# Routing of four batches in fuller loop steps, and a rule on when an expert slot may begin: top-k attention followed by a mixture of experts on one core

## The chip, the cores and the metric

One core of a Trainium2 chip runs one program. The metric is the device time of one execution in microseconds, as the median of several runs. The engines are named as the profile names them: PE (TensorE, matmuls; PEld its weight loads), DVE (VectorE), ACT (ScalarE), POOL (GpSimd), SP (SyncE, which here issues DMAs; SPq is its queue).

## The reference

Attention over 8 batches, 8 heads, 576 rows and 64 columns keeps the 32 highest scores of each row. Its output, as 4608 rows of 512, goes through a router and then, each row through one of 8 experts:

```python
scores = scale * np.matmul(q, k.transpose(0, 1, 3, 2))
kth = np.partition(scores, -top_k, axis=-1)[..., -top_k:-top_k + 1]
mask = scores >= kth
scores = np.where(mask, scores, -1000000000.0)
...
logits = x @ w_gate + modality_bias[modality_id]
e_idx = np.argmax(logits, axis=1)
...
    h = np.maximum(x[mask] @ w1[e], 0.0)
    out[mask] = gate_w[mask, None] * (h @ w2[e])
```

## The kernel before, in words

**The main loop.** The scores are cut into 288 tiles of 128 x 576 (a pair of heads has 9, a batch 36). A main loop of 310 steps, numbered i, is software-pipelined over the tiles. In step i PE makes the scores of tile i+2 (L396), ACT copies them to SBUF as Ssb (L404), DVE takes the eight largest of each of seven parts of tile i (MAX8, L411), merges those of tile i-1 (L420 to L424), and searches tile i-5 once more (`find`, L453) in the product y that POOL made of scores and signs (L449). From a count of signs and three small steps (L460 to L462) the 32nd value follows, and DVE's L473 (`keep`) makes the masked, unnormalised row P of tile i-7. Behind each L473 stands a gate on POOL (L477): a copy of one element of P, so that POOL starts the next y only when that L473 is over. PE transposes P (L488), ACT copies it (L496), and PE multiplies with V (L516).

**Routing.** When a batch's 36 tiles are done, its logits are made on PE and summed on DVE (L582 to L590). Then `route` (L592) gives a list of small steps: softmax and arg max on DVE (L627 to L635), ranks within the expert by a few small matmuls (L607 to L611), two products on POOL (L640, L641), the gate weight and the row's place in a sorted list on DVE (L642 to L646), then bookkeeping. POOL divides each row block by its softmax sum in halves (L556, 80 in all) and scatters each of the batch's five blocks of rows to the list xs in DRAM by an indirect DMA (L620, `SEND` below). `count_up` (L649) adds the batch's counts, `done` says that the batch is counted (`seen`).

The loop takes these steps from a queue `side`, at most `SN` = 4 to a loop step, and puts them behind that step's DVE work, each between two other instructions where there are any. A `PAUSE` in the queue ends the loop step's share, so that what follows stands in the next loop step. For the first `EB` batches the count comes before the scatters, which wait in `sendq` and leave one to a loop step; for the others the scatters come first and the count last. The two kinds also place logits and row blocks at different loop steps of the 36 (`RLF`, `RLM`, `RL` and `RXF`, `RXM`, `RX`, L1241).

**Expert slots.** A slot is 256 rows of one expert: rows xg are loaded from xs (L732), transposed (L791), multiplied with w1 (L803) and w2 (L815) and scattered to the output (L830, an indirect DMA on POOL). Which expert comes next is decided on the chip by some ten small DVE steps (L703 to L723). Where slots pause for want of counted rows, `more_moe` (L877) begins anew when a batch has been counted: it puts those picks, the w1 loads (L751), the xg load, three or two `PAUSE`s and the token step (L743 on DVE, or L740 on POOL) into a queue `rush`, of which at most `RN` = 6 go into a loop step. A slot's PE work (36 pieces) is dealt out over the loop steps by a budget in `spare_pe`: each step adds `STEP` = 3.3 and takes off what attention costs. Until the first slot begins, `keep_warm` (L928) gives PE dummy matmuls (L931). Slots that are not done in the loop follow behind it, in `slot` (L1005), with matmuls of another form.

SP issues its DMAs in the program's order: loads of k, q and v, the copies of ks and qs for the next pair of heads (L316, L318), weights and xg.

Of the kernel before, what the change touches and what calls it, by code (L numbers as in the profile page):

```python
# [26 lines left out]
SN = 4  # L27
# [23 lines left out]
PB = 6  # L51
COST = {"trans": 0.5, "qk": 0.5, "mix": 1.12, "rest": 0.22, "t": 0.11, "prep": 0.43, "logits": 1.2, "xrow": 0.54, "av": 0.42, "av8": 0.17}
RN = 6
QO = 0
EB = 3
RLF = (0, 1)
RXF = (3, 4, 5, 6, 7)
RLM = (3, 4)
# [12 lines left out]
def kernel(  # L71
# [14 lines left out]
    B, H, S, D = q.shape  # L86
# [4 lines left out]
    NT = NPAIR * 9  # L91
# [23 lines left out]
    PAUSE = lambda: None  # L115
# [284 lines left out]
    def sevac(i, parts=False):  # L400
        T[i]["S"] = sb = wk.tile([128, S], FT, name="Ssb", bufs=LR + 1 + QL - QO)
        sv = sb.rearrange("p (a b) -> p a b", a=2)
# [190 lines left out]
    def route(lg, bias, oh, x5b, early=False):  # L593

        t5 = lambda nm: const.tile([128, 5], FT, name=nm)
        t40 = lambda nm: const.tile([128, 5, E], FT, name=nm)
        bc = lambda t: t[:, :, None].to_broadcast([128, 5, E])
        be = lambda t: t[:, None, :].to_broadcast([128, 5, E])
        l2, z, key, ez, pr, pb = t40("r_l2"), t40("r_z"), t40("r_key"), t40("r_ez"), t40("r_pr"), t40("r_pb")
        mx, km, sm, ps5 = t5("r_mx"), t5("r_km"), t5("r_sm"), t5("r_ps5")  # L600
        dest = const.tile([128, 5], I32, name="dest")
        st = {}

        def ranks():
            ps = psX.tile([128, 6, E], FT, name="X")
            st["ps"] = const.tile([128, 6, E], FT, name="r_rk")
            PE.matmul(ps[:, 0:5, :], tri, oh, start=True, stop=False, skip_group_check=True)  # L607
            for c in range(1, 5):
                PE.matmul(ps[:, c:5, :], onesb, oh[:, 0:5 - c, :], start=False, stop=False, skip_group_check=True)
            for c in range(5):  # L610
                PE.matmul(ps[:, 5, :], onesb, oh[:, c, :], start=(c == 0), stop=(c == 4), skip_group_check=True)  # L611
            A.activation(st["ps"], ps, AF.Copy)

        def total():
            assert not behind
            V.tensor_reduce(ps5, pr, axis=AX.X, op=OP.add)

        def send(c):
            n_ = 128 if c < 4 else 64
            apart(G.indirect_dma_start(  # L620
                out=xs[:ZROW, :], out_offset=bass.IndirectOffsetOnAxis(ap=dest[:n_, c:c + 1], axis=0),
                in_=x5b[:n_, c, :], in_offset=None), scat, reads)
            if not early:
                fresh.append(scat[-1])

        return [
            lambda: V.tensor_tensor(l2, lg, bias, op=OP.add),  # L627
            lambda: V.tensor_reduce(mx, l2, axis=AX.X, op=OP.max),
            lambda: V.tensor_tensor(z, l2, bc(mx), op=OP.subtract),
            *[PAUSE] * EZP,  # L630
            lambda: A.activation(ez, z, AF.Exp),
            lambda: V.scalar_tensor_tensor(key, z, 0.0, be(rev), op0=OP.is_equal, op1=OP.mult),
            lambda: V.tensor_reduce(km, key, axis=AX.X, op=OP.max),
            lambda: V.tensor_tensor(oh[:, 0:4, :], key[:, 0:4, :], bc(km)[:, 0:4, :], op=OP.is_equal),
            lambda: V.tensor_tensor(oh[:64, 4, :], key[:64, 4, :], km[:64, 4:5].to_broadcast([64, E]),  # L635
                                    op=OP.is_equal),
            *[PAUSE] * RKP,
            ranks,
            PAUSE,
            lambda: on_pool(lambda: G.tensor_tensor(pb, st["ps"][:, 0:5, :], be(base), op=OP.add)),  # L640
            lambda: on_pool(lambda: G.tensor_tensor(pr, pb, oh, op=OP.mult)),  # L641
            lambda: V.tensor_reduce(sm, ez, axis=AX.X, op=OP.add),  # L642
            lambda: V.tensor_scalar(sm, sm, EPS, None, op0=OP.add),
            lambda: V.reciprocal(x5b[:, :, GW], sm),
            total,
            lambda: V.tensor_scalar(dest, ps5, float(ZROW), None, op0=OP.add),  # L646
            lambda: G.tensor_scalar(x5b[:, :, TOK], tokb, 1.0, 1.0, op0=OP.mult, op1=OP.mult),
            lambda: G.tensor_scalar(tokb, tokb, float(S), 1.0, op0=OP.add, op1=OP.mult),
        ], [lambda c=c: send(c) for c in range(5)], lambda: V.tensor_tensor(base, base, st["ps"][:, 5, :], op=OP.add)  # L649
# [208 lines left out]
    rush = deque()  # L858
    moe = deque()
    puts = deque()  # L860
    xev = deque()
    seen = [0]
    nslot = [0]
# [10 lines left out]
    plan = {"ready": -1, "go": False}  # L874
    quiet = set()

    def more_moe():  # L877

        n = nslot[0]
        b = seen[0] // S  # L880
        full = 2 * b
        fits = lambda x: x >= PB
        if plan["ready"] == n:
            if moe or not plan["go"]:
                return
            chores()
            nslot[0] += 1
            nxt = full >= n + 2
            moe.extend(expert(n, True, nxt, fits(n + 1), True))
            if nxt:  # L890
                plan.update(ready=n + 1, go=True)
        elif full >= n + 1:
            now = SL[n - 1] if moe else {"xt": True, "used": [4, 4]}
            if not now["xt"]:
                return
            plan.update(ready=n, go=False)
            pick, rows, done, tok = sched(n, fits(n))
            free = []

            def begin():  # L900
                free.extend(now["used"])
                now["nxt"] = True

            def take(x, g):
                return lambda: (load_w1, load_w2)[x](n, g) if g < free[x] else None
            l1 = [lambda: [take(0, g)() for g in range(4)]]
            l2 = [take(1, g) for g in range(4)]
            go = [lambda: plan.update(go=True)]
            lead = l1 + [WAIT] + rows if sendq else rows + l1
            rush.extend(pick + [begin] + lead + done + [PAUSE] * (3 if b < 2 else 2) + tok + go)  # L910
            quiet.update(l2)
            side.extend([f for x in l2 for f in (x, PAUSE)])
# [152 lines left out]
    for i in range(LAST):  # L1065
# [13 lines left out]
        if ok(i + QL):  # L1079
            cost += COST["mix" if (i + QL) % 9 == 8 else "qk"]  # L1080
        if QO == 0:
            scores()
# [12 lines left out]
        while nxt:  # L1095
            nxt.popleft()()
        if ok(i + QL) and QO == 0:
            sevac(i + QL)
# [20 lines left out]
        if 0 <= b1 < B:  # L1119
            if r == 0:  # L1120
                chore.extend(recip(b1, den[b1 % 2]))
            rl, rx = (RLF, RXF) if b1 in (0, B - 1) else (RLM, RXM) if b1 < EB else (RL, RX)
            if r == rl[0]:
                rows_of[b1] = logits(b1, xTs(b1))
                cost += COST["logits"]
            if r == rl[1]:
                logit_rows(b1, rows_of[b1], lgb[b1 % 2], later if 0 < b1 < EB else late)
                cost += COST["xrow"]
# [4 lines left out]
            def done(n=b1 + 1):  # L1133
                seen[0] = n * S
                fresh.clear()
            if r == rl[1] + (3 if 0 < b1 < EB else 2):
                steps, sends, count_up = route(lgb[b1 % 2], bias_all[:, b1], ohb[b1 % 2], x5, b1 < EB)
                side.extend(steps)
                if b1 < EB:
                    side.extend([count_up, done, lambda x=sends, n=5 * b1: sendq.extend((c, f, n + c) for c, f in enumerate(x))])  # L1140
            if b1 >= EB and r == max(rl[1], rx[4]) + 3:
                side.extend([f for x in sends for f in (x, PAUSE)] + [count_up, done])
# [7 lines left out]
        spare_pe = min(spare_pe + (STEP if i < NT + TL + END[0] else END[1]) - cost, CAP)  # L1150
        while seen[0] and spare_pe > 0:
            if i < NT + ME:
                more_moe()
            if not moe:
                break
            c, f, new = moe[0]
            if new and after:
                break
            moe.popleft()
            f()  # L1160
            spare_pe -= c
        if QO == 1:
            scores()
# [13 lines left out]
        for x, f in enumerate(lo):  # L1177
            b_.insert(LOP[x] if x < len(LOP) else len(b_), f)
        small_ = []
        for x in range(RN if rush else 0):  # L1180
            if rush and rush[0] is WAIT and sendq:
                break
            f = rush.popleft() if rush else PAUSE
            if f is PAUSE:
                break
            small_.append(f)
        if not small_:
            while bulk and not PJ[1] < j <= PJ[2]:
                chore.append(bulk.popleft())
            while chore:  # L1190
                small_.append(chore.popleft())
        for x in range(SN - len(small_)):
            if side and side[0] in quiet and PJ[1] < j <= PJ[2]:
                break
            f = side.popleft() if side and not rush else PAUSE
            if f is PAUSE:
                break
            small_.append(f)
# [208 lines left out]
```

## Time and profile before

| | |
|---|---|
| median of 3 runs | 1256.58 us (1254.93 to 1257.7) |
| the profiled execution | 1256.33 us |
| its span, first to last instruction | 1254.5 us |
| mean granted PE clock | 0.983 |
| busy, of the span | PE 1182.1 us (94%), DVE 1156.4 (92%), ACT 1018.0 (81%), POOL 687.8 (55%) |

A row of instructions in order of time has: start us, duration us, engine, line, operation, output<-inputs, shapes, count, and in brackets the engine's idle time before it and what ended it. A row that sums a line's instructions has their durations in ns as least/median/most and the first and last start in us. Busy time is not the same as time that counts: an engine that isn't waited for costs nothing, and an instruction that is held up by another engine's access shows as a long duration, not as idle time.

### The profile page before, as it was taken

What the parts mean: (1) busy time and instruction counts of PE and PEld (TensorE: products, weight loads), DVE (VectorE), ACT (ScalarE), POOL (GpSimd) and SP (SyncE); (2) the same over time, 40 slices, a digit from 0 to 9 for tenths busy, and PEclk for the clock granted to TensorE, in tenths of its full rate; (3) what the DMA queues carried; (4) which work ended last, traced back from release to release, by engine and by line L of the source; (5) the groups of instructions that cost most, each with busy time, mean ns of one, the idle gap of its engine ahead of it and who ended that gap; (6) DMA issues with size and microseconds to landing.
All of it is one profiled execution on the core that took longest, in us unless ns stands there. A gap on an engine that the chain in (4) does not pass through costs nothing. (4 is left out here: it accounts for less than half of the span.)

```text
span 1254.5 us, 29230 instructions
## 1 busy us (share of the span) xinstructions
PE 1182.1 (94%) x8141; PEld 929.6 (74%) x8141; DVE 1156.4 (92%) x5827; ACT 1018.0 (81%) x2042; POOL 687.8 (55%) x1342
## 2 busy tenths in 40 slices
PE   7888888899999999999999999999999999899995
PEld 6666676776868677786867777787868766799894
DVE  5999999999999999999999999999999995866764
ACT  4899988889989998988988988898889885555553
POOL 3555558456765576656865676556766772511110
PEclk8899998999999999999999999999999999999998
DMA  6665334775477557565476466666586423777563
GB/s 132 161 177 124 87 87 130 189 195 156 92 204 211 135 151 198 164 170 137 128 219 175 121 186 192 183 158 165 135 240 162 125 93 101 232 242 269 196 217 124
DMA packets 210133, 205.80 MB, mean 164 GB/s; under 512 B 106365, under 2 KB 155517, under 8 KB 209952
## 3 DMA queue, kind: packets, MB, share of 16 engines
q1 hardware_dynamic: 202384, 183.61, 54.1%
q0 software_dynamic: 6208, 19.54, 4.4%
q8 instruction: 70, 1.15, 0.4%
q14 instruction: 111, 0.91, 0.2%
q10 hardware_dynamic: 1360, 0.59, 0.2%
HBM read 123.35 MB, written 24.23 MB: 118 GB/s over the span
## 5 line engine op out<-in xcount | busy, mean ns | idle before, releaser
L411 DVE MAX8 cand<-Ssb 128x8 f32<-128x82 f32 (+1 forms) x2016 | 430.8, 231 | 8.9 <-ACT Ssb L404 8.9
L449 POOL TENSOR_TENSOR y<-Ssb,K 128x576 f32<-128x576 f32 x288 | 366.8, 1274 | 4.7 <-ACT K L443 4.1
L396 PE MATMUL S<-ks,qs 128*128 128x288 f32 x1016 | 232.9, 352 | 34.4 <-ACT Ssb L404 25.0
L404 ACT ACTIVATE Ssb<-S 128x576 f32<-128x576 f32 (+1 forms) x289 | 189.2, 655 | 72.0 <-PE S L396 53.0
L443 ACT ACTIVATE K<-Ssb,n 128x576 bf16<-128x576 f32 x288 | 227.8, 791 | 13.0 <-POOL y L449 12.5
L396 PEld LDWEIGHTS S<-ks,qs 128*128 128x128 f32 x1016 | 158.1, 193 | 91.9 <-issue 39.7
L467 ACT ACTIVATE ex<-Ssb,sm 128x576 f32<-128x576 f32 x288 | 226.1, 785 | 0.0
L453 DVE MAX8 mg<-y 128x8 f32<-128x576 f32 x288 | 214.6, 745 | 2.1 <-POOL y L449 2.1
L473 DVE SCALAR_TENSOR_TENSOR P<-Ssb,kth,ex 128x576 f32<-128x576 f32 x256 | 213.7, 835 | 0.6 <-PE T L488 0.3
L496 ACT ACTIVATE PT<-T 128x640 f32<-128x640 f32 (+1 forms) x288 | 191.5, 665 | 8.1 <-PE T L488 8.1
L803 PE MATMUL E<-xgT,w1b 128*128 128x256 f32 x768 | 188.3, 387 | 4.6 <-ACT xgT L784 2.4
L815 PE MATMUL E<-w2b,hT 128*128 128x512 f32 x384 | 182.7, 600 | 0.7 <-ACT hT L807 0.3
L488 PE MATMUL T<-idf,P 128*128 128x128 f32 x1152 | 170.1, 275 | 0.0
L803 PEld LDWEIGHTS E<-xgT,w1b 128*128 128x128 f32 x768 | 139.3, 191 | 31.1 <-ACT xgT L784 3.9
L477 POOL TENSOR_SCALAR spare<-P 1x1 f32<-1x1 f32 x256 | 47.8, 187 | 207.9 <-DVE mg L422 191.1
L516 PE MATMUL X<-PT,vm 128*64 128x256 f32 (+1 forms) x1536 | 147.8, 335 | 3.5 <-ACT st L279 2.5
L488 PEld LDWEIGHTS T<-idf,P 128*128 128x128 f32 x1152 | 136.5, 141 | 3.5 <-issue 1.3
L436 POOL TENSOR_SCALAR n<-mg 128x1 f32<-128x1 f32 x288 | 65.9, 229 | 109.1 <-DVE mg L424 100.8
L516 PEld LDWEIGHTS X<-PT,vm 128*64 128x64 f32 x1536 | 85.8, 137 | 50.4 <-issue 16.6
L815 PEld LDWEIGHTS E<-w2b,hT 128*128 128x128 f32 x384 | 66.5, 190 | 54.2 <-issue 50.5
L556 POOL TENSOR_TENSOR x<-x,rd 128x256 f32<-128x256 f32 (+1 forms) x80 | 53.8, 678 | 27.8 <-ACT x L560 27.8
L443 ACT ACTIVATION_READ_ACCUMULATOR K<-Ssb,n 128x1 f32 x288 | 61.5, 213 | 0.0
(208 smaller groups left out, 2248.7 us busy)
## 6 DMA issues: line engine op xcount, KB each, us to landing
w1b<-in_moe_w_dram SPq DMA_DIRECT2D x80, 512.0 KB, 5.6
w2b<-in_moe_w_dram SPq DMA_DIRECT2D x80, 512.0 KB, 5.6
ks<-st SPq DMA_DIRECT2D x64, 288.0 KB, 3.7
qs<-st SPq DMA_DIRECT2D x126, 144.0 KB, 2.9
ks<-st SPq DMA_DIRECT2D x62, 256.0 KB, 5.0
xg<-xs SPq DMA_DIRECT2D x20, 516.0 KB, 3.8
vm<-in_v_dram SPq DMA_DIRECT2D x32, 256.0 KB, 3.2
km<-in_k_dram SPq DMA_DIRECT2D x63, 128.0 KB, 4.1
```

Source lines behind the costliest of these rows:

```text
L396: PE.matmul(ps[:, hf, u - a:v - a], l, d["ks"][:, x, h, u + o:v + o], start=(n == 0), stop=(n == len(terms) - 1), skip_group_check=(j == 8))
L411: return [lambda s=s: V.max(c[:, s * 8:s * 8 + 8], T[i]["S"][:, bnd[s]:bnd[s + 1]]) for s in range(NSUB)]
L443: A.activation(t["K"], t["S"], AF.Sign, scale=2.0 ** -24 - 1.0, bias=t["n"][:, 1, i % 3:i % 3 + 1], accum_out=t["n"][:, 0, i % 3:i % 3 + 1])
L449: G.tensor_tensor(t["y"], t["S"], t["K"], op=OP.mult)
L453: V.max(t["mg"][:, i % 3, 24:32], t["y"])
L467: A.activation(t["ex"], t["S"], AF.Exp, bias=t["s"][:, i % 3:i % 3 + 1])
L473: V.scalar_tensor_tensor(t["P"], t["S"], kth[:, i:i + 1], t["ex"], op0=OP.is_ge, op1=OP.mult, accum_out=dn)
L488: PE.transpose(T[i]["pt"][:, x, :], (Pm if c == 4 else Pb[c % 2])[:, h * 512 + x * 128:h * 512 + x * 128 + 128], idf)
L496: A.activation(o, T[i]["pt"][:, :n], AF.Copy)
L516: PE.matmul(o.rearrange("p (a b) -> p a b", a=2) if j < 8 else o, l, r, start=(c == 0), stop=(c == 4), skip_group_check=True)
L803: PE.matmul(ps[:, f % 2], w1b[:, c, f * 128:(f + 1) * 128], xgT[:, c, :], start=(c == 0), stop=(c == KC - 1))
L815: PE.matmul(o["py"], hT[:, f, t * 128:(t + 1) * 128], w2b[:, f, :], start=(f == 0), stop=(f == FC - 1))
```

## The change

Five edits:

- `EB` goes from 3 to 4: batch 3, too, is counted before its scatters, and its logits and row blocks take the loop steps of batches 1 and 2.
- While fewer than `EB` batches are counted, a loop step takes up to `SF` = 8 routing steps in place of `SN` = 4.
- While fewer than `PB` = 6 slots have begun, it takes up to `RF` = 9 steps of `rush` in place of `RN` = 6.
- In the routing of those batches a `PAUSE` stands ahead of `total`, which reads what POOL made (the code asserts that POOL's part isn't still to be issued).
- `more_moe` gets a flag that is true from step 288 (`NT`), where the last scores have been made: no further slot begins in the loop then.

```diff
 RN = 6
+SF, RF = 8, 9
 QO = 0
-EB = 3
+EB = 4
...
             lambda: V.reciprocal(x5b[:, :, GW], sm),
+            *[PAUSE] * early,
             total,
...
-    def more_moe():
+    def more_moe(over):
...
-            if moe or not plan["go"]:
+            if moe or not plan["go"] or over:
                 return
...
-                more_moe()
+                more_moe(i >= NT)
...
-        for x in range(RN if rush else 0):
+        for x in range((RN if nslot[0] >= PB else RF) if rush else 0):
...
-        for x in range(SN - len(small_)):
+        for x in range((SN if seen[0] >= EB * S else SF) - len(small_)):
```

The changed file has one line more from L54 on and two from L646 on, so a line number below that is one or two higher than the same line's before.

How the instructions move, at three places. POOL in the routing of batch 0, over two loop steps (x is the block of rows, rd the inverse sums, r_rk the ranks, ohb the one-hot choice, n and spare the threshold's bias and the gate's target). Before:

```order
L449 TENSOR_TENSOR y<-Ssb,K 128x576
L640 TENSOR_TENSOR r_pb<-r_rk,tbl 128x40
L641 TENSOR_TENSOR r_pr<-r_pb,ohb_178 128x40
L556 TENSOR_TENSOR x_186<-x_186,rd 128x256 x2
L436 TENSOR_SCALAR n<-mg 128x1
L647 TENSOR_SCALAR x_186<-tokb 128x5
L477 TENSOR_SCALAR spare<-P_153 1x1
L449 TENSOR_TENSOR y<-Ssb,K 128x576
L556 TENSOR_TENSOR x_186<-x_186,rd 128x256 x2
L436 TENSOR_SCALAR n<-mg 128x1
L648 TENSOR_SCALAR tokb<-tokb 128x5
L477 TENSOR_SCALAR spare<-P_154 1x1
```

The same two loop steps (53 and 54) in the changed kernel:

```order
L450 TENSOR_TENSOR y<-Ssb,K 128x576
L557 TENSOR_TENSOR x_186<-x_186,rd 128x256 x2
L621 DMA xs<-x_186,dest 38912x516
L534 MEMSET spare 1x1
L437 TENSOR_SCALAR n<-mg 128x1
L478 TENSOR_SCALAR spare<-P_153 1x1
L450 TENSOR_TENSOR y<-Ssb,K 128x576
L557 TENSOR_TENSOR x_186<-x_186,rd 128x256 x2
L621 DMA xs<-x_186,dest 38912x516
L534 MEMSET spare 1x1
L437 TENSOR_SCALAR n<-mg 128x1
L478 TENSOR_SCALAR spare<-P_154 1x1
```

The two products stand one loop step earlier, and the first scatters now stand behind two divisions each; before, the first scatter came in step 55.

POOL in the routing of batch 1, loop step 93 (qbd are two fills for the next pair of heads). Before:

```order
L449 TENSOR_TENSOR y<-Ssb,K 128x576
L640 TENSOR_TENSOR r_pb<-r_rk,tbl 128x40
L641 TENSOR_TENSOR r_pr<-r_pb,ohb_179 128x40
L556 TENSOR_TENSOR x_186<-x_186,rd 128x256
L556 TENSOR_TENSOR x_186<-x_186,rd 64x256
L436 TENSOR_SCALAR n<-mg 128x1
L322 TENSOR_SCALAR qbd_145<-qs 128x64
L322 TENSOR_SCALAR qbd_146<-qs 128x64
L647 TENSOR_SCALAR x_186<-tokb 128x5
L477 TENSOR_SCALAR spare<-P_153 1x1
```

In the changed kernel:

```order
L450 TENSOR_TENSOR y<-Ssb,K 128x576
L557 TENSOR_TENSOR x_186<-x_186,rd 128x256
L557 TENSOR_TENSOR x_186<-x_186,rd 64x256
L621 DMA xs<-x_186,dest 38912x516
L534 MEMSET spare 1x1
L437 TENSOR_SCALAR n<-mg 128x1
L323 TENSOR_SCALAR qbd_145<-qs 128x64
L323 TENSOR_SCALAR qbd_146<-qs 128x64
L478 TENSOR_SCALAR spare<-P_153 1x1
```

A scatter has taken the place of the two products, in a loop step that also has two divisions and the two fills.

SP around the first slot's rows (w1b is a quarter of an expert's first matrix, sei the pick; TENSOR_LOAD and ISA read and set registers). Before:

```order
L751 DMA w1b<-in_moe_w_dram 128x4x256
L134 DMA km<-in_k_dram 128x4x64 x2
L140 DMA kqt<-in_k_dram 64x2x64
L134 DMA qm<-in_q_dram 128x4x64 x2
L140 DMA kqt<-in_q_dram 64x2x64
L731 TENSOR_LOAD sei_168
L731 ISA x2
L732 ISA
L732 DMA xg<-xs 128x1032
```

In the changed kernel, where the four w1b stand ahead of the first ks row:

```order
L317 DMA ks<-st 64x2x64
L319 DMA qs<-st 64x576 x4
L733 TENSOR_LOAD sei_168
L733 ISA x2
L734 ISA
L734 DMA xg<-xs 128x1032
L135 DMA km<-in_k_dram 128x4x64 x2
L141 DMA kqt<-in_k_dram 64x2x64
L135 DMA qm<-in_q_dram 128x4x64 x2
L141 DMA kqt<-in_q_dram 64x2x64
```

The load of xg has moved ahead of six loads of k and q.

## Rows read from the trace of the kernel before

**Rows 1.** Line L453: duration in ns least/median/most, first and last start.

```profile
L453 DVE MAX8 mg<-y x288: 729/745/761, 27.4 to 1046.0; 128x8 f32<-128x576 f32 x144
```

**Rows 2.** Stretches: length, busy PE, PEld, DVE, ACT, POOL, PE clock, DMA share, GB/s.

```profile
27.40:1046.00 1018.60, 973.41 (x6773) 748.89 (x6772) 1010.05 (x5430) 902.54 (x1858) 643.32 (x1241) 0.99 0.59 159
1046.00:1254.50 208.50, 189.27 (x1236) 164.26 (x1234) 132.62 (x308) 106.10 (x166) 37.54 (x74) 0.97 0.58 196
```

**Rows 3.** DVE's waits: us in total, times, longest us.

```profile
DVE cand L411 <- ACT Ssb L404: 8.9, 6, 4.6
...
DVE mg L453 <- POOL y L449: 2.1, 4, 0.8
```

**Rows 4.** Line L473.

```profile
L473 DVE SCALAR_TENSOR_TENSOR P<-Ssb,kth,ex x256: 787/802/2204, 34.6 to 1048.2; 128x576 f32<-128x576 f32 x128
```

**Rows 5.** DVE in order of time, routing of batch 1.

```profile
338.46 2.20 DVE L473 SCALAR_TENSOR_TENSOR P<-Ssb,kth,ex 128x576 f32<-128x576 f32 x1
```

**Rows 6.** POOL in order of time, the same moment.

```profile
338.20 1.27 POOL L449 TENSOR_TENSOR y<-Ssb,K 128x576 f32<-128x576 f32 x1
339.44 0.61 POOL L556 TENSOR_TENSOR x<-x,rd 64x256 f32<-64x256 f32 x1
```

**Rows 7.** Line L815, the slots' second matmuls in the loop.

```profile
L815 PE MATMUL E<-w2b,hT x384: 591/592/697, 270.8 to 1074.2; 128*128 128x512 f32 x192
```

**Rows 8.** Line L931, the dummy matmuls.

```profile
L931 PE MATMUL E<-idf,onesb x390: 272/273/437, 17.2 to 230.6; 128*128 128x256 bf16 x195
```

**Rows 9.** SP's DMA issues in order of time, around the first slot.

```profile
214.47 2.46 SPq L751 DMA_DIRECT2D w1b<-in_moe_w_dram  x4
217.04 2.01 SPq L134 DMA_DIRECT2D km<-in_k_dram  x2
...
225.14 0.37 SPq L732 DMA_DIRECT2D xg<-xs  x1
```

**Rows 10.** DVE in order of time, the first slot's token step.

```profile
228.82 0.17 DVE L743 COPY sgt<-xg 128x2 f32<-128x2 f32 x1 [1.23 <-DMA xg<-xs]
```

**Rows 11.** DVE in order of time, routing of batch 3.

```profile
599.85 1.93 DVE L473 SCALAR_TENSOR_TENSOR P<-Ssb,kth,ex 128x576 f32<-128x576 f32 x1
...
604.13 1.25 DVE L646 TENSOR_SCALAR dest<-r_ps 128x5 int32<-128x5 f32 x1
...
628.93 1.25 DVE L461 TENSOR_TENSOR jk<-eq,mg 128x27 f32<-128x27 f32 x1
```

**Rows 12.** DVE in order of time, routing of batch 1.

```profile
325.92 0.67 DVE L632 SCALAR_TENSOR_TENSOR r_key<-r_z,rev 128x40 f32<-128x40 f32 x1
326.51 0.17 DVE L461 TENSOR_TENSOR jk<-eq,mg 128x27 f32<-128x27 f32 x1
...
327.49 1.18 DVE L473 SCALAR_TENSOR_TENSOR P<-Ssb,kth,ex 128x576 f32<-128x576 f32 x1
```

**Rows 13.** DVE in order of time, routing of batch 2.

```profile
455.00 0.67 DVE L460 TENSOR_TENSOR eq<-i9s,n 128x27 f32<-128x27 f32 x1
455.60 0.67 DVE L632 SCALAR_TENSOR_TENSOR r_key<-r_z,rev 128x40 f32<-128x40 f32 x1
456.19 0.64 DVE L461 TENSOR_TENSOR jk<-eq,mg 128x27 f32<-128x27 f32 x1
...
464.80 1.08 DVE L473 SCALAR_TENSOR_TENSOR P<-Ssb,kth,ex 128x576 f32<-128x576 f32 x1
...
467.87 0.79 DVE L460 TENSOR_TENSOR eq<-i9s,n 128x27 f32<-128x27 f32 x1
```

**Rows 14.** POOL in order of time, routing of batch 0, from gate to gate.

```profile
196.16 0.18 POOL L477 TENSOR_SCALAR spare<-P 1x1 f32<-1x1 f32 x1
...
197.55 1.18 POOL L556 TENSOR_TENSOR x<-x,rd 128x256 f32<-128x256 f32 x2
198.91 1.11 POOL L620 DMA_INDIRECT xs<-x,dest  x1 [0.18 <-issue]
...
200.62 0.18 POOL L477 TENSOR_SCALAR spare<-P 1x1 f32<-1x1 f32 x1
```

## The prediction

> **What bounds the kernel now.** I read the stretches first, then the waits, then single lines in order of time. The main loop fills most of the span: the searches of L453, one per tile, run from 27.4 to 1046.0 us [rows 1], so 287 steps take 1018.6 us, 3.55 us each. In that stretch VectorE (DVE) is busy for 1010.05 of 1018.60 us and TensorE (PE) for 973.41 [rows 2]: DVE sets the pace, 8.6 us of the loop are its idle time, and no stage of the loop waits on PE for long. The 208.5 us behind it have DVE at 132.62 [rows 2]; they are the last expert slots. DVE's own waits in the loop are few: 8.9 us for scores' copies, up to 4.6 at once (the fill of the loop), 2.1 for POOL's product y [rows 3], and once 1.23 us for an xg load [rows 10]. So removing waits has little left to win. What can move is how long DVE's instructions last: L473 takes 0.79 to 2.20 us around a median of 0.80 [rows 4]. In the longest, at 338.46, POOL's y ran from 338.20 and a row division to 340.05, and L473 ended at 340.66 [rows 5, 6]: it stood still while POOL worked. The gate (L477) orders y behind L473; it fails when POOL is behind and starts y just in front of the next L473.
>
> **The change, part by part.** *No new slot from step 288 on.* Free, and it does nothing here. The twelfth slot fills the loop's end: its last matmuls of L815 start at 1074.2 us, behind the loop's last search at 1046.0 [rows 7, 1]. In the changed order the twelfth slot begins at step 281 instead of 280 and again empties its queue at step 307, outside the steps 288 to 298 for which the new test could act. So slots in the loop stay twelve, the same expert counts are seen at each pick, and the stage behind the loop is the same work.
>
> *Earlier counts.* Routing of batches 0 to 2 ends two loop steps sooner, of batch 3 twelve sooner. The first six slots begin 1 to 3 steps earlier, the last ones 0 to 2 later, since PE's budget per step is untouched. That alone pays nothing: DVE has the same instructions, and the loop is as long as they are. Two rounds of warm-up matmuls (12 of the 390 in L931, 0.27 us each [rows 8]) go; they stand on PE, beside a busy DVE, so 0.
>
> *The xg load of slot 0.* Before, SP issues it at 225.14, behind km, kqt and qm, which began at 217.04 [rows 9]; DVE's L743 waited 1.23 us for it [rows 10]. In the new order xg stands ahead of those six, and w1b ahead of the ks stacks. With 8 us of issue time gained and two steps (7.1 us) of earlier demand, I take the whole wait as gone: -1.2 us; the ends are 0 and -1.2. The price is that ks is issued later by the 2.46 us of the four w1b issues [rows 9], five steps (18 us) before its first matmul: 0.
>
> *Batch 3 routed like batches 0 to 2.* Its window now has three large stalls: L473 at 599.85 takes 1.93, L646 at 604.13 1.25 and L461 at 628.93 1.25 us [rows 11]. An undisturbed L473 takes 0.80 [rows 4] and a small step with two inputs 0.17 [rows 12]; so 1.1 + 1.1 + 1.1 = 3.3 us. The batches that have the early order already: batch 1 loses 1.4 [rows 5], 0.5 and 0.4 [rows 12], in all 2.3; batch 2 loses 0.5 in each of L460, L632 and L461, 0.6 in another L460 and 0.3 in L473 [rows 13], in all 2.4. Moving batch 3 from 3.3 to 2.4: -1.0 rounded; the ends are -3.3 and 0.
>
> *Fuller steps.* Eight routing steps or nine picks to a loop step in place of four or six. The number of DVE instructions is the same, so their issue time is 0 in the sum. But POOL's work moves together: a scatter (L620) now stands in the loop steps that still have two divisions. Such a step is in the trace once: from one gate at 196.16 to the next at 200.62, with two divisions of 1.18 and the scatter of 1.11 [rows 14] behind a y of 1.27 [rows 6], POOL takes 4.46 us, against 3.55 for a mean DVE step and some 0.1 us more for each small step in it. In the new order batch 0 has three of them where it had one, and batches 1 to 3 one each where they had none, with the two fills of qbd behind it: five more. Each leaves POOL behind by up to about 0.9 us, and what that costs DVE lies between 0 (POOL catches up: the step with nine picks is itself a microsecond longer) and the 1.4 us of [rows 5]. The row nearest is the one such step there is: no L473 of that step is held up, only small steps are, as in [rows 13], 0.5 us. I take 0.4 for each of five: +2.0, ends 0 and +7.0.
> Here a rule speaks against the change. The Trainium skill, page "SBUF — State Buffer", section "Who interferes with whom", says that a DVE instruction with two SBUF inputs and a GpSimd instruction that reads SBUF exclude each other for the whole instruction, and that whoever starts second is blocked to the end. The trace agrees for L473 at 338.46. By the rule every collision costs the rest of POOL's instruction, and this term would be +6 (the slower rival), not +2.
>
> *The sum:* -1.2 - 1.0 + 2.0 = **-0.2 us**. The profiled execution took 1256.33 us (span 1254.5 and 1.8 around it), which gives 1256.1; the median of the three runs is 0.25 above it, so 1256.4 is predicted. The terms' ends, -4.5 and +7.0, give the forecast alone some 1253 to 1259.5.
>
> **The rivals.** *Slower: POOL falls behind and y lands in front of L473.* In each of the five added steps, 4.46 us of POOL's work against a DVE step of 3.6 to 4.2, and in three of them some 0.5 more for qbd. The case decides where y starts within its own 1.27 us before the next L473. Then each costs about 1.2 (between 1.1 and 1.4 above): +6.0, with -1.2 and -1.0 it is +3.8, 1260.4 us. For it: 338.46 and 599.85 are just that. Against: steps with more small work are longer on DVE too, and the one full step of before kept its L473.
> *Faster: the longer steps free the gate.* If the steps with eight or nine small instructions give POOL time to catch up, the stalls at 338.46, 599.85 and 604.13 or 628.93 go (1.4 + 1.1 + 1.1), the wait for xg goes (1.2), and nothing comes in: -4.8, 1251.8 us. For it: batch 3's divisions, spread over many steps now, end sooner. Against: POOL's total is the same in a shorter stretch.
> *The change moves nothing that lasts.* The slots' shift by one or two steps only reshuffles where output scatters meet the gate; 0, 1256.6 us. It is inside the forecast.
>
> **How the numbers follow.** A measurement of this kernel tells a change from none at about 0.2%, 2.5 us: below 1254.1 is faster, above 1259.1 slower. Forecast and no-effect case together 0.53, of which 0.46 lie within 2.5 us, 0.04 below and 0.03 above; the faster rival 0.25, the slower 0.22. So faster 0.29, same 0.46, slower 0.25. The range 1251.8 to 1260.8 reaches to both rivals' times and leaves about 2 in 10 beyond them.
>
> **What would show it.** Right: no wait of L743 near 220 us; L931 with 378 matmuls; 12 slots' L815 in the loop as before; the loop's searches ending within 2.5 us of where they did; L473 with about as many values above 1 us. Wrong: waits of L453 for y in the four routing windows, or L473 at 2 us in three or more of the steps with two divisions and a scatter (slower); no L473 or small step above 1 us up to 640 us (faster). A stage behind the loop that is longer or shorter than 208 us by more than 1 us, or new waits for scores' copies after 30 us, would contradict the whole account.

## The result, and the profile after

The changed kernel takes **1264.3 us** (median of 5 runs, 1262.43 to 1266.0) against 1256.58 before: ratio 1.0070, 95% interval 1.0054 to 1.0086. It is slower by about 0.7%. The prediction, 1256.4 us in a range of 1251.8 to 1260.8, was wrong, and the true time lies outside the range.

The profiled execution took 1266.0 us with a span of 1264.2. Its loop and the stage behind it (columns as in [rows 2]):

```profile
25.50:1053.20 1027.70, 973.81 (x6759) 746.69 (x6759) 1016.86 (x5430) 901.84 (x1858) 645.93 (x1241) 0.99 0.59 157
1053.20:1264.20 211.00, 190.88 (x1236) 165.41 (x1234) 132.86 (x308) 105.83 (x166) 36.94 (x74) 0.97 0.57 193
```

Beside [rows 2]: the loop is 9.1 us longer. DVE has the same 5430 instructions, but they are busy for 6.8 us more (1016.86 against 1010.05), and the other 2.3 us are idle time of DVE. PE's busy time is the same within 0.4 us. The stage behind the loop is 2.5 us longer here, and this is not put down to the change: in this execution PE's granted clock falls there from 2.4 to 1.2 GHz for 3.4 us, at 1103.1 us. Of the variants below, the four whose profile has such a fall between 1076 and 1100 us (e4 to e7) are 0.6 to 1.5 us over the kernel before in that stage, and the six without it between 0.5 us under and 0.2 over.

The lines that answer to [rows 1, 4, 8], and DVE's waits in the loop, where [rows 3] had 8.9 and 2.1:

```profile
L454 DVE MAX8 mg<-y x288: 729/745/764, 25.5 to 1053.2; 128x8 f32<-128x576 f32 x144
...
L474 DVE SCALAR_TENSOR_TENSOR P<-Ssb,kth,ex x256: 786/803/1637, 32.7 to 1055.4; 128x576 f32<-128x576 f32 x128
...
L933 PE MATMUL E<-idf,onesb x378: 272/273/437, 16.9 to 223.8; 128*128 128x256 bf16 x189
```

```profile
DVE cand L412 <- ACT Ssb L405: 7.5, 6, 4.6
...
DVE lt L588 <- PE X L580: 1.4, 1, 1.4
DVE mg L454 <- POOL y L450: 1.4, 3, 0.6
```

L474's longest is 1.64 us (L473 had 2.20 before), and waits for y fell. What the slower rival named is not there. New is the wait of L588, the step that reads a batch's logits, for PE.

To find the place, the loop is cut by its searches, so that each stretch holds the same work of the main chain in every kernel: the n-th search of one kernel is put against the n-th of another. Difference of each stretch's length to the kernel before, in us, worked out from those starts (first search counted as step 5):

| kernel | 5 to 47 | 47 to 140 | 140 to 178 | 178 to 236 | 236 to 262 | 262 to 276 | 276 to 292 | loop |
|---|---|---|---|---|---|---|---|---|
| before (length) | 138.7 | 336.9 | 135.7 | 208.8 | 94.7 | 49.6 | 54.2 | 1018.6 |
| after | +0.1 | +9.3 | +1.3 | -3.9 | -1.7 | +4.0 | 0.0 | +9.1 |
| e1_eb4 | 0.0 | -1.1 | +5.8 | 0.0 | -1.5 | +4.0 | +0.3 | +7.5 |
| e2_fuller | -0.1 | +6.1 | -1.8 | -1.3 | -1.2 | +5.0 | +0.3 | +7.1 |
| e5_late | 0.0 | -1.7 | -0.6 | +5.5 | -1.4 | +4.0 | +0.4 | +6.2 |
| e6_early | 0.0 | +7.9 | +1.3 | -3.1 | -0.7 | 0.0 | -0.1 | +5.4 |
| e7_hold | +0.1 | +6.1 | +1.2 | -4.2 | -1.9 | +5.7 | +0.3 | +7.2 |
| e8_dest | 0.0 | +4.4 | +0.8 | -3.5 | -1.8 | +4.0 | +0.4 | +4.2 |
| e9_eb4_mended | +0.1 | -1.1 | -0.6 | +0.3 | -0.7 | 0.0 | 0.0 | -2.0 |
| e10_fuller_early | +0.1 | +8.9 | -1.8 | -0.9 | -0.7 | 0.0 | 0.0 | +5.6 |

Two losses stand out in the changed kernel: +9.3 in the routing of batches 0 to 2 (steps 47 to 140), and +4.0 in steps 262 to 276, where no part of the change seems to be: there batch 6 is routed, as it was before. One profiled execution can lie 5 us off its kernel's median (e6's took 1262.38 us, the median is 1257.23), so the table says where, and the times of many runs say how much.

**The late loss.** The stretches from step 236 to 262 in two pieces and from 262 to 276, of the kernel before:

```profile
847.52:900.21 52.69, 52.19 (x344) 40.38 (x344) 51.65 (x262) 47.52 (x100) 39.14 (x75) 1.00 0.64 169
900.21:942.23 42.02, 42.02 (x281) 30.00 (x280) 41.74 (x236) 36.81 (x77) 24.52 (x49) 1.00 0.68 195
942.23:991.85 49.62, 48.58 (x343) 39.00 (x342) 49.35 (x273) 44.67 (x95) 29.98 (x61) 1.00 0.58 146
```

The same three of the changed kernel:

```profile
852.39:903.78 51.39, 50.10 (x327) 37.66 (x326) 51.15 (x262) 45.62 (x97) 39.19 (x75) 1.00 0.65 173
903.78:945.41 41.63, 41.63 (x255) 29.58 (x254) 41.35 (x232) 33.75 (x70) 23.38 (x47) 1.00 0.64 181
945.41:999.05 53.64, 52.34 (x387) 42.08 (x386) 51.77 (x278) 49.64 (x107) 33.92 (x66) 1.00 0.55 139
```

Read the counts of matmuls: 344, 281 and 343 became 327, 255 and 387, so 43 left the first two stretches and 44 came into the third. The last three slots in the loop begin at steps 243, 261 and 281 in the changed order and began at 241, 259 and 280 before, but only some seven of these matmuls are the slots' own; the others are nearly all attention's transposes, products with V and scores. The stretches are cut by DVE's searches, and what has moved is PE's place against them. PE begins the scores of loop step 262 (first row: before, second: after), whose search DVE starts at 942.23 and 945.41:

```profile
940.81 0.77 PE L396 MATMUL S<-ks,qs 128*128 128x288 f32 x4
```

```profile
947.31 0.77 PE L397 MATMUL S<-ks,qs 128*128 128x288 f32 x4
```

Before, PE was 1.4 us ahead of the search; now it is 1.9 us behind. From the scores of step 236 to these it has 609 matmuls in either kernel, but takes 94.9 us in place of 92.1, with four w2b matmuls more, four transposes of xg fewer and 0.8 us more idle time. In the next 14 loop steps the slots have 80 matmuls in either kernel. So PE comes into the third stretch with more still to do. There it was busy for 48.58 of 49.62 us already; now it is busy for 3.76 us more, and the stretch grew by 4.0. On DVE the 4.0 are 1.6 us of idle time and 2.4 us of busy time (278 instructions against 273); POOL's work for the slots moved with the shift too (33.92 us busy against 29.98), and its part was not taken apart. The 1.7 us that DVE gained in the two stretches ahead don't make up for it. The wait is in DVE's order of time, kernel after; the same step of the kernel before stands behind it without a wait:

```profile
975.38 0.29 DVE L588 TENSOR_TENSOR lt<-X,rd 128x128 f32<-128x128 f32 x1 [1.45 <-PE X L580]
```

```profile
969.18 0.28 DVE L587 TENSOR_TENSOR lt<-X,rd 128x128 f32<-128x128 f32 x1
```

Behind this wait the routing steps of batch 6 also meet POOL at worse moments: L644, a step that took 0.25 us there in the kernel before, takes 1.26 us.

**The routing loss.** DVE and POOL in order of time, routing of batch 3 in the kernel after:

```profile
600.14 0.18 DVE L617 TENSOR_REDUCE r_ps<-r_pr 128x5 f32<-128x40 f32 x1
600.35 2.49 DVE L648 TENSOR_SCALAR dest<-r_ps 128x5 int32<-128x5 f32 x1
602.76 0.23 DVE L412 MAX8 cand<-Ssb 128x8 f32<-128x83 f32 x1
```

```profile
600.38 1.27 POOL L450 TENSOR_TENSOR y<-Ssb,K 128x576 f32<-128x576 f32 x1
601.63 1.19 POOL L557 TENSOR_TENSOR x<-x,rd 128x256 f32<-128x256 f32 x2
603.12 1.06 POOL L621 DMA_INDIRECT xs<-x,dest  x1 [0.31 <-DVE dest L648]
```

L648 turns 128x5 row places into integers, 0.15 us of work. It is held from the moment y begins until the second division ends (602.82), and everything on DVE stands behind it. The scatter comes after L648 and waits for it, so it isn't the scatter that blocks. The line as a whole, against 152/170/1250 of its eight before (their longest is in [rows 11]):

```profile
L648 DVE TENSOR_SCALAR dest<-r_ps x8: 153/495/2490, 188.5 to 1081.1; 128x5 int32<-128x5 f32 x8
```

In batch 2 other small steps are held instead, by y and a division from 473.64 on and by y at 478.07:

```profile
473.92 1.61 DVE L719 TENSOR_SCALAR s_ft<-pos,s_sc 128x2 f32<-128x2 f32 x1
...
478.29 1.10 DVE L720 TENSOR_SCALAR smk<-pos,s_sc 128x2 f32<-128x2 f32 x1
```

Of the 9.3 us in steps 47 to 140, 7.9 are DVE's own busy time (341.69 against 333.79 us, 1820 instructions against 1821). L648 has 2.3 of them, the threshold's small step L461 has 2.4, and the picks have most of the rest.

**A wait for qs, in steps 104 to 122.** In the changed order three loads of w2b (an expert's second matrix) stand on SP ahead of the copies of qs for the next pair of heads; before, they stood behind them. Kernel before, then kernel after:

```profile
372.99 3.37 SPq L318 DMA_DIRECT2D qs<-st  x4
376.60 2.25 SPq L755 DMA_DIRECT2D w2b<-in_moe_w_dram  x4
```

```profile
372.78 2.72 SPq L757 DMA_DIRECT2D w2b<-in_moe_w_dram  x3
375.62 2.60 SPq L319 DMA_DIRECT2D qs<-st  x4
```

PE waits for these copies. Its order of time in the kernel after, then the same place in e2_fuller, whose edits are the same but for the fourth batch:

```profile
384.85 0.76 PE L397 MATMUL S<-ks,qs 128*128 128x288 f32 x4 [3.01 <-DMA qs<-st]
...
386.00 4.44 PE L805 MATMUL E<-xgT,w1b 128*128 128x256 f32 x12
```

```profile
386.01 0.77 PE L397 MATMUL S<-ks,qs 128*128 128x288 f32 x4 [1.50 <-DMA qs<-st]
...
387.16 2.76 PE L805 MATMUL E<-xgT,w1b 128*128 128x256 f32 x12
```

In the kernel after, the granted clock falls from 2.4 to 1.2 GHz behind the wait, for the 3.4 us from 386.30 on, and the twelve matmuls take 4.44 us in place of 2.76:

```profile
386.30:389.70 3.40, 3.40 (x10) 2.66 (x9) 3.40 (x21) 2.02 (x5) 1.87 (x4) 0.50 0.87 248
```

The profiles of e3, e6, e7 and e10 have this wait too (1.89 to 3.30 us) and a fall of the clock beside it; in these four and the changed kernel steps 104 to 122 are 0.3 to 2.7 us longer than before. Those of e2 and e8 (no wait) have no fall, and there these steps are 1.2 and 1.8 us shorter. e10 and e2 have the same program up to step 232 and differ by 2.7 us here: about that much of the +9.3 comes with the wait and the clock, and not from POOL. No run moved these loads alone.

**The wait for xg** of [rows 10] is gone, as predicted (a later slot waits 0.4 us). SP and DVE in order of time, kernel after:

```profile
215.89 0.36 SPq L734 DMA_DIRECT2D xg<-xs  x1
216.34 1.28 SPq L135 DMA_DIRECT2D km<-in_k_dram  x2
```

```profile
220.73 0.15 DVE L745 COPY sgt<-xg 128x2 f32<-128x2 f32 x1
```

### The profile page after: what moved, and what is told of

Same layout as the page of the kernel before. It is cut to its first block, busy times and chain, and to the rows that moved or that the text cites. A ratio compares the mean times of both kernels' runs of the same rounds, so it can differ in the third digit from the quotient of the medians.

```text
span 1264.2 us, 29207 instructions
## 1 busy us (share of the span) xinstructions
PE 1183.0 (94%) x8129; PEld 927.6 (73%) x8129; DVE 1163.4 (92%) x5827; ACT 1016.9 (80%) x2042; POOL 689.8 (55%) x1342
## 5 line engine op out<-in xcount | busy, mean ns | idle before, releaser
L474 DVE SCALAR_TENSOR_TENSOR P<-Ssb,kth,ex 128x576 f32<-128x576 f32 x256 | 213.3, 834 | 2.3 <-ACT ex L468 1.2
L437 POOL TENSOR_SCALAR n<-mg 128x1 f32<-128x1 f32 x288 | 70.3, 244 | 110.8 <-DVE mg L425 102.5
L817 PEld LDWEIGHTS E<-w2b,hT 128*128 128x128 f32 x384 | 66.4, 190 | 54.0 <-issue 49.6
```

What stands on the lines that cost most here:

```text
L474: V.scalar_tensor_tensor(t["P"], t["S"], kth[:, i:i + 1], t["ex"], op0=OP.is_ge, op1=OP.mult, accum_out=dn)
L817: PE.matmul(o["py"], hT[:, f, t * 128:(t + 1) * 128], w2b[:, f, :], start=(f == 0), stop=(f == FC - 1))
```

## The experiments

The kernel before was run again beside the variants, with medians of 1255.16 to 1255.42 us; the ratios are to these runs.

| kernel | what it is | median us | ratio, 95% interval |
|---|---|---|---|
| e1_eb4 | before, only `EB` = 4 | 1263.91 | 1.0064 (1.0047 to 1.0082) |
| e2_fuller | after, `EB` = 3 | 1263.48 | 1.0062 (1.0047 to 1.0078) |
| e3_rf6 | after, six picks to a step | 1267.26 | 1.0090 (1.0074 to 1.0107) |
| e4_sf4 | after, four routing steps to a step | 1267.86 | 1.0093 (1.0077 to 1.0109) |
| e5_late | before, slots 10 to 12 at steps 243, 261, 281 | 1259.24 | 1.0023 (1.0009 to 1.0037) |
| e6_early | after, slots 10 to 12 at steps 241, 259, 280 | 1257.23 | 1.0018 (1.0004 to 1.0033) |
| e7_hold | after, no division beside the row places | 1260.61 | 1.0044 (1.0027 to 1.0060) |
| e8_dest | after, the row places by another form | 1260.25 | 1.0031 (1.0013 to 1.0050) |
| e9_eb4_mended | e1, five pauses, slots early | 1253.18 | 0.9984 (0.9970 to 0.9998) |
| e10_fuller_early | e2, slots early | 1259.88 | 1.0033 (1.0018 to 1.0048) |

**The parts alone.** First the two halves of the change, apart.

```diff
 # before
-EB = 3
+EB = 4
```

> The kernel before with the fourth batch counted ahead of its scatters, and nothing else (EB = 4; four and six steps to a loop step as before). Theory P (the loss is in the fuller steps: POOL's scatter, divisions and y come to stand beside DVE's row places L646 and first picks L703 and hold them up): no loss, 1254 to 1257 us, since batch 3 gives up its own three stalls of 3.3 us and the two or three new ones cost less. Rival B (the loss comes from the fourth early count and the slots that it shifts): 1260 us or more.

```diff
 # after
-EB = 4
+EB = 3
```

> The changed kernel with three batches counted early in place of four (EB = 3; eight and nine steps, the pause, the slot rule kept). Theory P: three of the four crowded routings stay, at some 2 us each, so 1261 to 1263 us. Rival B: the loss goes, 1256 to 1258 us.

Each half alone costs as much as both together: 1263.91 and 1263.48. e1 has rival B's time, so the loss is not in the fuller steps alone; e2 lies just above theory P's. The halves do not add, and what is common to both has to be looked for. Common is the shift of slots 10 to 12, to 243, 261 and 281 in both, and +4.0 (e1) and +5.0 (e2) in steps 262 to 276. What e1 has beside it is one wait of another kind. Its SP and POOL in order of time:

```profile
612.73 7.58 SPq L751 DMA_DIRECT2D w1b<-in_moe_w_dram  x3
623.36 6.57 SPq L316 DMA_DIRECT2D ks<-st  x6
630.79 0.36 SPq L732 DMA_DIRECT2D xg<-xs  x1
```

```profile
634.70 0.19 POOL L740 TENSOR_SCALAR sgt<-xg 128x2 f32<-128x2 f32 x1 [7.78 <-DMA xg<-xs]
...
635.15 1.26 POOL L449 TENSOR_TENSOR y<-Ssb,K 128x576 f32<-128x576 f32 x1
```

SP issues xg behind w1b and ks, whose issues take 7.58 and 6.57 us there; the token step on POOL reaches L740 first and stands for 7.78 us; the gate and y stand behind it on POOL, and DVE waits 5.5 us for y. That is 5.5 of the +5.8 us in steps 140 to 178. In the changed kernel, with fuller steps, the loads come in time and this wait is absent.

**Which of the two densities.** Then the picks and the routing steps, one undone at a time.

```diff
-SF, RF = 8, 9
+SF, RF = 8, 6
```

> The changed kernel with six steps of a new slot's picks to a loop step in place of nine (RF = 6). Theory P: the row places L648 stay in the crowded loop step (0.8, 1.3 and 2.0 us of stall in the changed trace), so most of the loss stays: 1261 to 1264 us. Rival A (small dependent steps that stand next to each other on DVE cost latency; nine are worst): the loss falls by half or more, 1257 to 1260 us.

```diff
-SF, RF = 8, 9
+SF, RF = 4, 9
```

> The changed kernel with four routing steps to a loop step in place of eight (SF = 4; nine picks kept). Theory P: the row places stand in a loop step without a scatter again, as before; what stays is the nine picks beside the first scatters: 1256 to 1259 us. Rival A: the nine picks still cost their latency: 1260 us or more.

Both are slower than the whole change, which no theory had expected. What their profiles have more of is DVE's wait for xg, here in e3 and then in e4, against 1.2 us in all before and 0.4 in the changed kernel:

```profile
DVE sgt L745 <- DMA xg<-xs: 5.7, 2, 5.1
```

```profile
DVE sgt L745 <- DMA xg<-xs: 13.3, 3, 6.6
```

In e4 SP issues the first xg at 227.99 us, in the changed kernel at 215.89. So eight routing steps and nine picks belong together: the token step's place in the order is fixed by steps, the load's by when the count and the pick are through and SP gets to it. In e4 the row places are free again (L648 least/median/most 149/162/486 ns, against 2490 at most with eight steps), as the theory of the crowding had it; its time was missed for the waits. Steps 47 to 140 are +12.0 there, +15.1 in e3.

**The slots' shift by itself.** PE's budget loses 2.0 us in step 223 of the kernel before, which delays slots 10 to 12, and gains 1.5 in step 232 of the changed kernel, which brings them to their old steps. No instruction is added or left out.

```diff
 # before
+        spare_pe -= 2.0 * (i == 223)
         while seen[0] and spare_pe > 0:
```

> The kernel before, where at loop step 223 a budget of 2.0 is taken off what PE may spend on the running slot, so that slots 10, 11 and 12 begin at steps 243, 261 and 281 as in the changed kernel and in the four variants, not at 241, 259 and 280; nothing else. Theory L (the late slots' shift of one or two steps puts their PE and POOL work beside the routing of batch 6): steps 262 to 276 take 4 to 5 us longer, as in all five slower traces, steps 236 to 250 about 1.2 shorter, and the time is 1258 to 1260 us. Rival P (what counts is the routing windows alone, the late stretch is chance): within 1.5 us of before.

```diff
 # after
+        spare_pe += 1.5 * (i == 232)
         while seen[0] and spare_pe > 0:
```

> The changed kernel, where at loop step 232 a budget of 1.5 is given to PE, so that slots 10, 11 and 12 begin at steps 241, 259 and 280 as before; nothing else. Theory L: the 4.0 us of steps 262 to 276 go and the 1.3 us gained in steps 236 to 250 go with them: 2.5 to 4 us less than the changed kernel, 1260 to 1262 us. Rival P: no change, 1263 to 1266 us.

Steps 262 to 276 in e5 and then in e6:

```profile
942.14:995.79 53.65, 52.36 (x387) 42.10 (x386) 51.79 (x278) 49.65 (x107) 33.86 (x66) 1.00 0.54 139
```

```profile
947.79:997.43 49.64, 48.87 (x347) 39.32 (x346) 49.37 (x273) 44.87 (x97) 30.03 (x61) 1.00 0.58 146
```

The kernel before, with late slots, has the stretch of the changed kernel to 0.01 us and to the matmul; the changed kernel with early slots has that of the kernel before. PE begins the scores of step 262 1.9 us behind the search in e5 and 1.1 us ahead of it in e6, so its place follows the slots' shift both ways. By the runs the shift costs 0.23% in e5 (2.9 us; 1.1 to 4.6 by the interval), and its removal gives 0.52% in e6 (1.0070 to 1.0018, 6.5 us; about 3.8 to 9.2) and 0.29% in e10 below, against e2 (3.6 us). The sizes differ, the sign and the place do not. (The +5.5 of e5 in steps 178 to 236 lies mostly ahead of step 223, where nothing had been changed: in that execution PE waits 3.9 us for qs until 670.6, and the granted clock falls to 1.2 GHz for 3.4 us from 671.5 on.)

**The crowded steps.** e7 lets POOL make no division in the loop step of an early batch's row places; e8 makes the row places with an instruction that also sums them (the sum isn't used).

```diff
-            lambda: V.tensor_scalar(dest, ps5, float(ZROW), None, op0=OP.add),
+            lambda: (early and hold.append(1), V.tensor_scalar(dest, ps5, float(ZROW), None, op0=OP.add)),
...
-        for _ in range(min(len(divide), 2 if len(divide) > 2 else 1)):
+        for _ in range(0 if hold else min(len(divide), 2 if len(divide) > 2 else 1)):
...
+        hold.clear()
```

> The changed kernel without POOL's divisions in the one loop step of an early batch in which the row places L648 are made (they follow in the next steps; the scatter stays in that step). If y and the divisions hold L648 up: its durations in the routing of batches 0, 1 and 3 (0.9, 1.45 and 2.2 us in the changed trace) fall by the divisions' 0.6 to 1.2 us each, and some of it returns in the next step, where the divisions now meet the first picks; 1 to 3 us less in all. If the scatter holds it up, L648 stays as long.

```diff
-            lambda: V.tensor_scalar(dest, ps5, float(ZROW), None, op0=OP.add),
+            lambda: V.tensor_scalar(dest, ps5, float(ZROW), 0.0, op0=OP.add, op1=OP.add, accum_out=dsum),
```

> The changed kernel with the row places L649 (here L649) made by the form of the same instruction that also writes a sum, in all batches; the rest as it is. If what holds L648 up is access shared with POOL that this form doesn't use: it takes under 0.4 us everywhere, and the four routing windows are 2 to 4 us shorter in all. If it is held up for another reason (its input comes late, or POOL's instruction blocks any form), it stays at 0.9 to 2.2 us.

The row places in e7, then, in the second fence, in e8 with the count's step that follows them:

```profile
L648 DVE TENSOR_SCALAR dest<-r_ps x8: 149/276/1323, 188.2 to 1079.0; 128x5 int32<-128x5 f32 x8
```

```profile
L649 DVE TENSOR_SCALAR_CACHE_REDUCE dest<-r_ps x8: 136/159/160, 190.0 to 1077.8; 128x5 int32<-128x5 f32 x8
...
L652 DVE TENSOR_TENSOR tbl<-tbl,r_rk x8: 144/299/2240, 190.3 to 1077.9; 128x8 f32<-128x8 f32 x8
```

Without divisions L648 waits for y alone (1.32 at most); in the other form it never waits (0.16 at most). But the stall passes on: in e8 the next step with two inputs, L652, is held for up to 2.24 us (0.35 in the changed kernel), in e7 the first pick, L705, for 1.54 (0.97). Both are faster than the change (1260.61 and 1260.25 against 1264.3), with no part of the shift undone, but these rows explain little of it: in e8 L649 and L652 take 5.8 us in batches 0, 1 and 3, where L648 and L651 took 6.0 in the changed kernel, and in e7 L648 is 3.4 us shorter there, and the first picks L705 of batches 0 to 3 are 2.3 us longer. e8's profile also lacks the wait for qs and the fall of the clock; whether the edit does that is not shown.

**The two mends together.** e9 is e1 with the slots back at their steps, and with five pauses in place of two ahead of the token step of the slots begun when four batches are counted (`b == EB`), so that xg lands first. e10 is the fuller steps with three early batches and slots back at their steps: the crowding without the shift.

```diff
 # before
-EB = 3
+EB = 4
...
-            rush.extend(pick + [begin] + lead + done + [PAUSE] * (3 if b < 2 else 2) + tok + go)
+            rush.extend(pick + [begin] + lead + done + [PAUSE] * (3 if b < 2 else 5 if b == EB else 2) + tok + go)
...
+        spare_pe += 1.5 * (i == 232)
```

> The kernel before with the fourth batch counted early (EB = 4, four and six steps), and the two losses that the trace of that variant showed taken out: five pauses in place of two ahead of slot 6's token step (there POOL waited 7.8 us for xg, whose load stood on SP behind w1b), and 1.5 of PE budget at loop step 232, so that slots 10 to 12 begin at 241, 259 and 280. Theory L and W (shift and wait are the whole loss of the fourth early count): 5.4 and 4.0 of its 8 us go, 1252 to 1256 us, at or a little under the kernel before. Rival B (the fourth early count costs by itself): 1259 us or more.

```diff
 # after
-EB = 4
+EB = 3
...
+        spare_pe += 1.5 * (i == 232)
```

> Fuller steps for three batches (EB = 3; eight and nine steps, the pause) and the slots' shift undone by 1.5 of PE budget at loop step 232. What is left against the kernel before is the crowding in the routing of batches 0 to 2 alone. By the stretches of the variant without the budget: +0.3 (steps 47 to 86), +3.4 (86 to 104), +3.6 (122 to 140), less some 3 between: 1258 to 1260 us, 3.5 to 5 us under that variant. If the shift were not what costs in the late stretch: 1262 us or more.

e9 is the only version ahead of both kernels: 1253.18 us, 0.9984 (0.9970 to 0.9998), an interval that only just leaves out 1. Against e1 that is 0.80%, 10 us, where the wait (5.5) and the shift (4.0) were to be won; the two mends were not run apart. Its loop (columns as above) is 2.0 us shorter than that of [rows 2], with the y waits of e1 gone:

```profile
26.29:1042.93 1016.64, 968.14 (x6771) 744.97 (x6771) 1007.76 (x5430) 901.11 (x1858) 644.25 (x1241) 1.00 0.59 159
```

e10 puts the fuller steps of three batches, without the shift, at 0.33% of 1255.4, 4.1 us; the gain at xg and the wait for qs are in this. In its profile steps 47 to 140 lose 8.9 us, and 3.4 come back up to step 262.

The test that lets no slot begin from step 288 on was not run by itself: leaving it out changes no engine's order of instructions, neither with three nor with four early batches. That is read from the written program, not measured.

## Why the prediction was wrong

**The step that failed first** is "*Earlier counts*": the last slots begin "0 to 2 later", and "That alone pays nothing: DVE has the same instructions, and the loop is as long as they are." The shift was seen and costed at 0. It cost 4.0 us in steps 262 to 276, and 2.9 us (e5) to 6.5 us (e6) by the runs. Behind the step stood a reading of the loop as a whole, that DVE sets the pace and "no stage of the loop waits on PE for long". The mean over 1018 us hid that PE, at 85% in steps 5 to 47 and 91% in 47 to 86, is busy for 98 to 100% of every stretch from step 86 to 276, and for 42.02 of 42.02 us in steps 250 to 262. Where both engines are full, a shift of PE's work is not neutral: it left PE 3.3 us later against the searches at step 262, and DVE paid for that in the next stretch. The rows of the kernel before, cut into stretches, could have been read so ahead of the prediction.

**The term that was mis-sized** is "*Fuller steps*", +2.0 with an upper end of +7.0. By the table steps 47 to 140 lose 9.3, 7.9 and 8.9 us (after, e6, e10) with the clock's fall and 6.1 (e2) without it, the gain of 1.2 at xg already taken off. By time the fuller steps of three batches cost 4.1 us (e10), again with that gain taken off: more than twice the term, which was for four batches, and inside its ends. The mechanism was right in the main, POOL's work standing in DVE's way. The price was taken from a row in which a small step lost 0.5 us; in the new order L648 alone loses 1.1, 1.6 and 2.3 us in batches 0, 1 and 3 (1.25, 1.78 and 2.49 us against 0.15 undisturbed; the kernel before had 0.56, 0.15 and 1.25), because y and the divisions follow on each other and the held step waits for them all. The argument that L473 would not be held more was right as well (11 above 1 us against 12 before, the longest 1.64 against 2.20), and it was the wrong place to look.

Here the rule of the Trainium skill that the prediction weighed is nearer than the price that was taken: page "SBUF — State Buffer", section "Who interferes with whom". It also lists `tensor_scalar` among the operations that can contend with GpSimd, where their operands meet further conditions, and excepts the form that writes out its accumulator; the trace agrees, with 2.49 us for L648 and 0.16 us for the accumulating form in e8. The page speaks of one whole instruction of the other engine. Here the measured block was longer: 2.49 us, over y (1.27) and both divisions (1.19).

**A cost that was looked for at one place only.** For the first slot the loads that now stand ahead of ks and qs were priced at 0, and there that is about right: PE waits 1.16 us for qs until 217.1, where it had waited 1.65 us for kqt until 226.8. The next pair's qs, behind w2b, was not looked at; there PE waits 3.01 us and the granted clock falls.

**Batch 3 routed early**, -1.0: not shown by any run. In the changed kernel the old stalls of L473 and L461 shrink in steps 140 to 178 (2.4 us less on L474 and L462), but L648 and the first picks take 2.2 us more there. In e9, where the xg wait and the shift are mended, these steps are 0.6 us shorter, but so they are in e5, which routes batch 3 as before. Of e9's 2.0 us in the loop, 1.1 lie in steps 47 to 140, where batch 3 is not routed yet, and 0.7 in steps 236 to 262, which e6 and e10 have as well. The times (e9 0.16% ahead, 0.02 to 0.30%) allow for the gain and don't say where it lies.

**Right**: the wait for xg (-1.2) and its reason, the load's place ahead of the k and q loads; the twelve dummy matmuls (378 of L933); a slot rule that does nothing, by the written program. Of the signs named for the forecast, the searches ended 7.2 us later than they did, where 2.5 were allowed. Of the signs of "wrong", none named PE; a stage behind the loop more than 1 us longer did come, but with the clock's fall of that one execution.

**The rivals.** The slower one, 1260.4 us, had POOL falling behind. Its price was near what e10 measures (1259.88), but its place was L473 and waits of L453, and neither came: the nearness is luck. The third rival has the slots' shift, at 0. The range ended at 1260.8, although the terms' own ends, -4.5 and +7.0, come to 1252.1 and 1263.6 about 1256.6, not to the "1253 to 1259.5" that the prediction gives.

**Open.** The runs put different sizes on the shift (2.9, 3.6 and 6.5 us), and why PE needs 2.8 us more for the same number of matmuls in steps 236 to 261 was not taken apart further. Steps 140 to 236 together are 2.6 to 3.0 us shorter than before in the changed kernel, e2 and e10, so with three early batches as with four; the cause was not looked for. The order of w2b and qs was not tried by itself.

## What to carry to other kernels

Where two engines are both near full, read the busy time stretch by stretch before costing a shift of "the other" engine's work at nothing: here a shift of one or two loop steps cost 4.0 us in one stretch and gave back 1.7 in the two ahead of it. A count of instructions in a stretch that another engine's work cuts out shows which engine runs ahead, too, and not only what was moved. When work is packed into fewer steps, look for the first instruction that shares a resource with the packed engine, and price it at that engine's whole run of work; an edit that relieves this one instruction can pass the wait to the next. When a part is tried alone, look first for loads that now come behind their reader on an issuing queue: three variants here lost 5.5 to 13.3 us of DVE's time in waits for one, and one of them, with this and the shift mended, is the only version that is faster.

## What was not expected of the hardware

A step of 128x5 elements with one tensor input (L648) was held for 2.49 us by work on POOL, where its accumulating form ran in 0.136 to 0.160 us in the same place, all eight times. And the hold went on over three POOL instructions in a row (600.38 to 602.82), not only to the end of the one that was running.
